# Three small rearrangements in a tuned linear-attention and feed-forward kernel: one state update earlier, one product and one mask moved to other engines

## The chip, the cores and the metric

The kernel runs on one core of a Trainium2 chip. The metric is the device time of one execution in microseconds (us). The profiler's span is some 1.7 to 1.9 us shorter than that time; spans are compared with spans and times with times. All executions here are of the state called fast (in the record their mean granted clock lies between 0.991 and 1.000). The engines are named as the profile names them: PE (TensorE matmuls), PEld (its weight loads), DVE (VectorE), ACT (ScalarE), POOL (GpSimd), and SP, whose queue (SPq) issues the DMA transfers.

## The reference, cut to what matters

```python
# batch 4, 8 heads, 768 positions, head_dim 64; causal linear attention with a decay per head
for b in range(nb):
    intra = einsum('bhic,bhjc->bhij', qb, kb) * Dmask          # scores inside the block, masked
    intra = einsum('bhij,bhjd->bhid', intra, vb)
    inter = einsum('bhid,bhde->bhie', qb * lam_pow, kv_state)  # earlier blocks, through the state
    out[:, :, sl] = intra + inter
    kv_state = lam_block * kv_state + einsum('bhsd,bhse->bhde', kb * rev_pow, vb)
# then a bilinear feed-forward on x = out, 3072 tokens of 512: (x @ w_a * (x @ w_b)) @ w_out, d_ff = 1536
```

## The kernel before

The 3072 tokens are cut into 24 units of 128 (6 per batch entry). For each unit the kernel multiplies q and k by decay factors (into a tile `qk`), transposes them (`qkT`; on PE up to unit 10, by a DMA transpose from unit 11), takes scores `kq`, masks them (`m`), adds intra and inter parts in PSUM (`o_ps`) and evacuates the sum as `xT`, the input of the feed-forward. The feed-forward runs over groups of 4, 1, 2, 4, 4, 4, 4 and 1 units, numbered from 0; while PE works on a group, a plan drops pieces of later units' attention into numbered slots between its matmuls. The order on every engine is fixed by the program.

```python
GROUPS = (4, 1, 2, 4, 4, 4, 4, 1)
PLAN = { ...
    2: [(0, "V", 6), (1, "T", 7), (1, "P", 8), (4, "T", 8), (5, "P", 9), (6, "S", 7),
        (6, "S", 8), (7, "V", 7), (8, "P", 10), (10, "T", 9), (11, "T", 10),
        (12, "Q", (7, 8, 9, 10)), (12, "P", 11), (13, "V", 9), (14, "P", 12),
        (14, "O2", (9, 10))],
    3: [(3, "S", 11), (3, "S", 12)], ... }
# groups 3, 4, 5 (u = 11, 15, 19): (1,"P",u+2) (3,"P",u+3) (4,"V",u) (7,"Q",(u,..,u+3)) (10,"P",u+4) ...
# P prepares a unit, T transposes on PE, S scores and masks, V updates the state,
# O2/Q finish two units (Q also takes the scores of two more)

def prep_k(u):
    early = u < n0 + 3                              # n0 = 4
    make_ks(u, "dve" if early else "pool")          # k times decay
    make_qs(u, "pool")                              # q times decay
    used["u"] = u + 1                               # lets pump() issue loads up to three units ahead
    if u >= DMA_T_FROM:                             # 11
        qkT = qkT_pool.tile(...)
        nc.sync.dma_start_transpose(out=qkT..., in_=U[u]["qk"]...)   # in the SP queue, in program order

def pieces_O(us, nxt=()):                           # O2 and Q
    ...inter(u) for us; scores(u) for nxt; intra(u) and evac_o(u) for us...
    if len(us) == 2 and us[0] >= n0 + 3:
        kv_beside(us[1])                            # eight half-width matmuls into the one state bank
    for u, kq in zip(nxt, kqs):
        masks(u, kq)                                # DVE, four masks
    if len(us) == 2 and us[0] >= n0 + 3 and us[1] % NB < NB - 1:
        kv_copy(us[1], kv["ps"])                    # DVE, behind the masks
```

## Time and profile before

| | before |
|---|---|
| median of the 3 runs given with it | 236.69 us (236.5 to 237.27) |
| median of 6 runs, with the 3 measured beside the changed kernel | 236.56 us (236.32 to 237.27) |
| span of the profiled execution | 234.5 us |
| PE, DVE, ACT, POOL busy | 96%, 49%, 40%, 21% |
| PE waits on lines that the change touches | 0.9 us (state copy), 0.3 us (ab product) |

The table is read with one question in mind: an engine other than PE matters only where PE waits for it. The columns are start, busy time, engine, line, operation, output from inputs, tile and shape, and the number of instructions; an idle time ahead of a row would follow in brackets.

```profile
99.75 1.03 PE L428 MATMUL b_ps<-xT,wb_sb 128*128 128x512 bf16 x4
100.62 0.39 PE L336 MATMUL o_ps<-qkT,st 128*128 128x128 bf16 x4
100.94 0.62 PE L309 MATMUL kq<-qkT 64*128 64x128 bf16 x16
101.49 0.64 PE L346 MATMUL o_ps<-m,vb 128*64 128x128 bf16 x16
```

The sixteen scores at 100.94 belong to units 13 and 14 and read what two DMA transposes wrote. No idle time is noted, so both had landed. By how much is not in this view: a list of waits shows only the transfers that came too late, never those that were just in time. The margin can be asked for. Unit 14's transpose was issued here:

```profile
94.87 2.20 SPq L281 DMA_TRANSPOSE qkT<-qk  x1
```

The view of the tile qkT for the stretch from 94.5 to 96 us gives 6.2 us from issue to landing, so it landed near 101.1. PE came to unit 14's scores, the second eight of the sixteen, at 101.17: the margin was below 0.1 us.

### The profile page before, as it was taken

What the parts mean: (1) busy time and instruction counts of PE and PEld (TensorE: products, weight loads), DVE (VectorE), ACT (ScalarE), POOL (GpSimd) and SP (SyncE); (2) the same over time, 40 slices, a digit from 0 to 9 for tenths busy, and PEclk for the clock granted to TensorE, in tenths of its full rate; (3) what the DMA queues carried; (4) which work ended last, traced back from release to release, by engine and by line L of the source; (5) the groups of instructions that cost most, each with busy time, mean ns of one, the idle gap of its engine ahead of it and who ended that gap; (6) DMA issues with size and microseconds to landing.
All of it is one profiled execution on the core that took longest, in us unless ns stands there. A gap on an engine that the chain in (4) does not pass through costs nothing.

```text
span 234.5 us, 4593 instructions
## 1 busy us (share of the span) xinstructions
PE 226.2 (96%) x1798; PEld 125.8 (54%) x1798; DVE 115.6 (49%) x205; ACT 92.9 (40%) x174; POOL 48.6 (21%) x63
## 2 busy tenths in 40 slices
PE   7699999999999899999999999999999999999994
PEld 2474444459688554454544454544454544444493
DVE  0896557637459644874144574135574224332050
ACT  3576753066463532242143242242341233431161
POOL 6041000254345453130333330030300000000000
PEclk9999999999999999999999999999999999999999
DMA  4999999999999999999819959515040220000311
GB/s 155 300 285 348 347 366 289 295 213 272 230 244 187 224 198 250 210 161 240 177 48 219 184 73 238 143 64 115 0 48 0 89 87 7 0 3 3 131 48 45
DMA packets 94278, 38.31 MB, mean 163 GB/s; under 512 B 81201, under 2 KB 89777, under 8 KB 94257
## 3 DMA queue, kind: packets, MB, share of 16 engines
q1 hardware_dynamic: 94112, 38.02, 72.1%
q8 instruction: 14, 0.23, 0.4%
q14 instruction: 8, 0.06, 0.1%
q10 hardware_dynamic: 144, 0.00, 0.0%
HBM read 28.32 MB, written 6.29 MB: 148 GB/s over the span
## 4 chain that ended last, share of the span: by engine, by line
PE 90%; DMA 3%; ACT 3%; DVE 2%; issue 1%; SPq 1%; DVEq 0%; ACTq 0%
PE a_ps L428 27%; PE b_ps L428 26%; PE op L449 26%; DMA k<-in_k_dram 3%; PE kq L309 2%; PE o_ps L346 2%; PE o_ps L336 2%; PE kvd L360 1%; PE tps L295 1%; ACT xT L353 1%; ACT o_sb L444 1%; DVE m L321 1%; SPq L207 1%; ACT st L390 1%; PE kq L561 1%
## 5 line engine op out<-in xcount | busy, mean ns | idle before, releaser
L440 DVE TENSOR_TENSOR ab<-a_sb,b_ps 128x512 bf16<-128x512 bf16 (+2 forms) x96 | 52.6, 553 | 80.6 <-PE b_ps L428 58.6
L428 PE MATMUL a_ps<-xT,wa_sb 128*128 128x512 bf16 (+2 forms) x384 | 77.1, 326 | 0.9 <-ACT xT L353 0.6
L428 PE MATMUL b_ps<-xT,wb_sb 128*128 128x512 bf16 (+2 forms) x384 | 77.2, 326 | 0.0
L435 ACT CAST a_sb<-a_ps 128x512 bf16<-128x512 f32 (+2 forms) x96 | 45.6, 481 | 63.5 <-PE a_ps L428 62.0
L449 PE MATMUL op<-wo_sb,ab 128*128 128x512 bf16 (+2 forms) x312 | 65.6, 363 | 0.0
L428 PEld LDWEIGHTS <-wb_sb 128*128 128x128 bf16 x384 | 34.5, 98 | 28.7
L428 PEld LDWEIGHTS <-wa_sb 128*128 128x128 bf16 x384 | 33.8, 98 | 29.4 <-issue 0.9
L449 PEld LDWEIGHTS <-ab 128*128 128x128 bf16 x312 | 28.7, 98 | 29.8
L321 DVE TENSOR_TENSOR m<-kq,lotri 128x512 bf16<-128x512 f32 x48 | 29.9, 683 | 19.3 <-PE kq L309 18.8
L257 POOL TENSOR_TENSOR qk<-kf,lp_k 128x512 bf16<-128x512 f32 x17 | 18.0, 1061 | 77.5 <-issue 31.6
L444 ACT COPY o_sb<-op 128x512 f32<-128x512 f32 (+2 forms) x26 | 14.2, 554 | 37.9 <-PE op L449 37.9
L262 POOL TENSOR_TENSOR qk<-qf,lp_q 128x512 bf16<-128x512 f32 x20 | 21.7, 1083 | 23.0 <-DMA qf<-in_q_dram 23.0
L353 ACT CAST xT<-o_ps 128x512 bf16<-128x512 f32 x23 | 12.5, 590 | 17.5 <-PE o_ps L346 17.4
L392 DVE TENSOR_TENSOR st<-kvd,bdiag 128x512 bf16<-128x512 f32 x18 | 12.3, 684 | 4.9 <-PE kvd L360 3.8
L297 ACT COPY qkT<-tps 128x1024 bf16<-128x1024 bf16 x7 | 7.1, 1012 | 10.4 <-PE tps L295 10.4
L195 PE MATMUL idle<-idle_sb 128*128 128x128 bf16 (+1 forms) x34 | 7.2, 348 | 1.3 <-DVE idle_sb L190 1.3
L271 DVE CAST vb<-vf 128x512 bf16<-128x512 f32 x17 | 8.3, 490 | 0.0
L271 POOL CAST vb<-vf 128x512 bf16<-128x512 f32 x7 | 4.8, 681 | 16.0 <-DMA vf<-in_v_dram 16.0
L346 PE MATMUL o_ps<-m,vb 128*64 128x128 bf16 x192 | 7.9, 222 | 0.0
L336 PEld LDWEIGHTS <-st 128*128 128x128 bf16 x80 | 5.4, 98 | 2.8
L309 PE MATMUL kq<-qkT 64*128 64x128 bf16 x160 | 6.6, 218 | 0.0
L346 PEld LDWEIGHTS <-vb 128*64 128x64 bf16 x192 | 5.8, 109 | 1.4
(54 smaller groups left out, 84.0 us busy)
## 6 DMA issues: line engine op xcount, KB each, us to landing
vf<-in_v_dram SPq DMA_DIRECT2D x24, 256.0 KB, 5.0
out_dram<-o_sb SPq DMA_DIRECT2D x23, 256.0 KB, 2.2
qf<-in_q_dram SPq DMA_DIRECT2D x20, 256.0 KB, 4.7
kf<-in_k_dram SPq DMA_DIRECT2D x20, 256.0 KB, 5.1
wst<-in_moe_w_a_dram SPq DMA_DIRECT2D x6, 512.0 KB, 8.7
wst<-in_moe_w_b_dram SPq DMA_DIRECT2D x6, 512.0 KB, 8.8
wst<-in_moe_w_out_dram SPq DMA_DIRECT2D x6, 512.0 KB, 8.5
q<-in_q_dram SPq DMA_DIRECT2D x2, 512.0 KB, 5.5
```

The source lines that it names most:

```text
L257: eng_of(eng).tensor_mul(qk[:, 1], raw.pop((u, "k")), lp_k[:, u % NB].to_broadcast([128, H, D]))
L262: eng_of(eng).tensor_mul(U[u]["qk"][:, 0], raw.pop((u, "q")), lp_q[:, u % NB].to_broadcast([128, H, D]))
L271: eng_of(eng).tensor_copy(vb, vf)
L321: nc.vector.tensor_mul(m, kq[i], lotri_bc)
L346: nc.tensor.matmul(d["o"][p, hp, :], lhsT=d["vb"][:, 2 * hp + i, :], rhs=d["m"](i, hp), start=(first and hp == 0), stop=True, skip_group_c ...
L353: nc.scalar.copy(xT[:, :, col:col + BLK], o_ps)
L392: nc.vector.tensor_mul(st[:].rearrange("p hp i d -> p hp (i d)"), ps[:].rearrange("p hp i d -> p hp (i d)"), bdiag_bc)
L428: nc.tensor.matmul(ps[:, :gt], lhsT=w_sb[:, s, f * 128:(f + 1) * 128], rhs=xT[:, s, :gt], start=(s == 0), stop=(s == KS - 1))
L435: nc.scalar.copy(a_sb[:, :gt], ps[:, :gt])
L440: nc.vector.tensor_mul(ab[:, f, :gt], a_sb[:, :gt], ps[:, :gt])
L444: nc.scalar.copy(o_sb[:, lo:hi], op[:, lo:hi])
L449: nc.tensor.matmul(op[:, lo:hi], lhsT=ab[:, f, t * 128:(t + 1) * 128], rhs=wo_sb[:, f, lo:hi], start=(f == 0), stop=(f == FC - 1))
```

## The change

The intent: PE waits in group 2 because unit 8's state copy stands behind four masks on DVE, so unit 8 gets its update alone, two slots earlier; in group 1 unit 6's k product leaves DVE; and in the opening one of eight masks is spread over ACT and POOL, unit 1's result is evacuated by DVE instead of ACT, and three idle-filling matmuls go.

```diff
--- before.py
+++ after.py
@@ -44,7 +44,7 @@
     1: [(0, "V", 4), (2, "T", 5), (3, "PK", 6), (6, "PV", 6), (6, "S", 5), (7, "T", 6),
         (10, "S", 6), (12, "O2", (5, 6)), (13, "P", 7)],
     2: [(0, "V", 6), (1, "T", 7), (1, "P", 8), (4, "T", 8), (5, "P", 9), (6, "S", 7),
-        (6, "S", 8), (7, "V", 7), (8, "P", 10), (10, "T", 9), (11, "T", 10),
+        (6, "S", 8), (7, "V", 7), (8, "P", 10), (10, "T", 9), (10, "V", 8), (11, "T", 10),
         (12, "Q", (7, 8, 9, 10)), (12, "P", 11), (13, "V", 9), (14, "P", 12),
         (14, "O2", (9, 10))],
     3: [(3, "S", 11), (3, "S", 12)],
@@ -272,8 +272,7 @@
         U[u]["vb"] = vb
 
     def prep_k(u):
-        early = u < n0 + 3
-        make_ks(u, "dve" if early else "pool")
+        make_ks(u, "dve" if u < n0 + 2 else "pool")
         make_qs(u, "pool")
         used["u"] = u + 1
         if u >= DMA_T_FROM:
@@ -314,11 +313,16 @@
         ms = mask(kq)
         U[u]["m"] = lambda i, hp: ms[i][:, hp, :]
 
-    def mask(kq):
+    def mask(kq, split=False):
         ms = []
         for i in range(2):
             m = msk_pool.tile([128, HP, 128], BF16, name=f"m{i}", tag=f"m{i}")
-            nc.vector.tensor_mul(m, kq[i], lotri_bc)
+            if split and i == 1:
+                raw_kq = scr[0][:, 8:9, :].rearrange("p s (h j) -> p (s h) j", h=HP)
+                nc.scalar.copy(raw_kq, kq[i])
+                nc.gpsimd.tensor_mul(m, raw_kq, lotri_bc)
+            else:
+                nc.vector.tensor_mul(m, kq[i], lotri_bc)
             ms.append(m)
         return ms
 
@@ -412,11 +416,11 @@
             intra(u)
             xT, col = xTs[u]
             evac_o(u, xT, col)
-        if len(us) == 2 and us[0] >= n0 + 3:
+        if len(us) == 2 and us[0] >= n0 + 5:
             kv_beside(us[1])
         for u, kq in zip(nxt, kqs):
             masks(u, kq)
-        if len(us) == 2 and us[0] >= n0 + 3 and us[1] % NB < NB - 1:
+        if len(us) == 2 and us[0] >= n0 + 5 and us[1] % NB < NB - 1:
             kv_copy(us[1], kv["ps"])
 
 
@@ -564,7 +568,7 @@
                                          start=True, stop=True, skip_group_check=True)
             kqs.append(kq)
         for up, kq in zip(ups, kqs):
-            ms4[i, up] = mask(kq)
+            ms4[i, up] = mask(kq, split=(i == 1 and up == 1))
 
     for u in range(n0):
         U[u] = dict(kn=kn4[:, u], qT=xT4["q"][:, :, u * BLK:(u + 1) * BLK],
@@ -579,7 +583,8 @@
     for at, i, j in ((2, 0, 0), (3, 0, 1), (4, 1, 0)):
         scale4("k", i, j)
         part_k(i, j, at)
-        warm(3)
+        if i == 0:
+            warm(3)
     scale4("k", 1, 1)
     for u in range(n0):
         make_vb(u, "pool")
@@ -608,7 +613,7 @@
     evac_o(0, *xTs[0])
     intra(1, True)
     inter(1)
-    evac_o(1, *xTs[1])
+    evac_o(1, *xTs[1], eng="dve")
     intra(2, True)
     intra(3, True)
     inter(2)
```

## The prediction

> **What bounds the kernel now.** I read the page first, then the waits of the tensor engine, then busy time by stage, then the timeline around each wait. The page puts PE far ahead of the rest, and the chain that ended last is almost all PE:
>
> ```profile
> PE 226.2 (96%) x1798; PEld 125.8 (54%) x1798; DVE 115.6 (49%) x205; ACT 92.9 (40%) x174; POOL 48.6 (21%) x63
> ...
> PE 90%; DMA 3%; ACT 3%; DVE 2%; issue 1%; SPq 1%; DVEq 0%; ACTq 0%
> ```
>
> So work taken from DVE, ACT or POOL is worth nothing by itself. Only three things shorten the run: PE work removed, a PE wait removed, or an earlier start of the steady part. The table by stage (stretch and its length, then busy us and instruction count of PE, PEld, DVE, ACT and POOL) says where waits are left:
>
> ```profile
> 0.00:18.73 18.73, 15.06 (x183) 9.56 (x184) 11.94 (x21) 10.77 (x20) 7.32 (x23) 1.00 0.95 253
> ...
> 51.92:62.90 10.98, 10.71 (x164) 8.82 (x164) 6.67 (x19) 6.13 (x17) 3.54 (x4) 1.00 1.02 254
> 62.90:86.15 23.25, 22.39 (x263) 17.29 (x262) 15.54 (x30) 11.45 (x22) 12.14 (x12) 1.00 1.15 208
> 86.15:212.80 126.65, 126.65 (x838) 62.26 (x837) 57.87 (x94) 42.78 (x74) 20.52 (x20) 1.00 0.59 113
> ```
>
> From 86 to 213 us PE has no gap at all, so a microsecond won before 86 should arrive at the end untouched. Before that the waits of PE are few, and two of them sit on lines that the change touches (columns: total us, times, longest):
>
> ```profile
> PE kvd L360 <- DVE st L392: 0.9, 1, 0.9
> ...
> PE a_ps L428 <- ACT xT L353: 0.6, 2, 0.5
> ...
> PE a_ps L428 <- DVE ab L440: 0.3, 1, 0.3
> ```
>
> The chain in order of time (start, length, what) shows each. In the opening, three idle-filling matmuls stand directly ahead of the scores; later four state copies and three xT casts on ACT stand ahead of the first feed-forward matmul:
>
> ```profile
> 11.47 0.17 PE idle L195 x3
> 11.64 0.55 PE kq L561 x16
> ...
> 17.08 1.60 ACT xT L353 x3
> 18.68 0.04 issue
> 18.73 1.89 PE a_ps L428 x8
> ...
> 55.54 0.40 DVE qk L257
> ...
> 56.14 0.29 DVE ab L440
> ...
> 80.16 1.28 DVE m L321 x2
> 81.44 0.61 DVE st L392
> 82.05 0.04 issue
> 82.09 0.38 PE kvd L360 x4
> ```
>
> At 55.5 us unit 6's k on DVE stands between two ab products, and PE waits for the second. At 82.1 us unit 9's state update waits until DVE has done four masks (units 9 and 10) and only then unit 8's state copy, which holds the one state bank.
>
> [...] POOL's k products have a mean of 1061 ns and its q products 1083. [...] the vb cast on DVE takes 421 ns at the median and 822 at most, and the timeline shows the 0.8 us ones beside a POOL product. [...] The trace shows only 112 ns against 98 per load in the half-width update, and eight of those cost PE about what four full-width ones cost (both 0.22 us, below).
>
> **The change, part by part.**
>
> Opening. The three idle matmuls go: 0.17 us from the chain. The DMA that landed k at 10.30 and the DVE scaling behind it do not move, so everything from the scores on moves by 0.17. DVE then does seven masks in place of eight. They follow each other every 0.61 us (eight take 4.88 from 12.07), so the seventh starts near 15.5 and ends near 16.2, and unit 2's state copy runs from about 16.15 to 16.8 instead of 16.87 to 17.55. The eighth mask goes ACT then POOL: the ACT copy (0.59 for this shape) fits in ACT's 0.99 us idle time before the first state copy, near 14.4 to 15.0; POOL is free at 15.66 after the fourth vb cast, whose DMA does not move, and multiplies until about 16.7. PE reaches the first matmul that reads this mask near 16.8, so it is just in time. ACT then has two xT casts instead of three; the last, unit 3's, now waits for PE's own inter matmuls (end 18.05 before, 17.88 here) and ends near 18.5 instead of 18.68. The first weights are cast by POOL until 17.76 + 0.62 = 18.38, held by a DMA, so no more than 0.3 can be won here. Gain: **0.2 us**.
>
> Unit 6's k to POOL. It takes 0.69 us from DVE and adds 1.05 to POOL, which is idle for 2.06 us from 51.8 and 1.37 from 54.5. POOL would do k and q of unit 6 by about 54.5, and PE's transposes want them at 56.9. The ab product moves from 56.14 to about 55.6. PE's scores before it start at 55.81 and take 0.33 in the chain, so the next matmul could start at 56.14 instead of 56.48. Gain: **0.34 us** (0.27 of it shown as idle, the rest is the refill of the pipeline, where the chain has 0.38 for the first four matmuls against 0.22 for later ones).
>
> Unit 8's update alone at slot 10. Added there: four full-width matmuls; for unit 7 the chain shows these as 0.22 us. Removed at slot 12: eight half-width ones, between 79.55 and the next matmul at 79.77, so 0.22. The PE work cancels. The state copy (0.68 us on DVE) moves from behind the masks to near 76.6, where DVE has caught up with PE and waits 0.24 us for the next product. Unit 9's update can then start when PE has issued its six matmuls from 79.77: 6 x 0.216 = 1.30, so at 81.07 instead of 82.09. Gain: **1.0 us at most**. What may be given back: after the masks DVE has unit 11's vb cast and then unit 9's copy, which the next inter needs near 82.8; if POOL starts unit 13's k, released by the same unit-9 update, just ahead of that cast, [...]. By the two gains upstream DVE comes 0.5 us earlier while unit 13's data land when they did, so I think DVE wins; I take off 0.15.
>
> Sum: 0.2 + 0.34 + 0.85 = 1.4 us. 236.69 - 1.4 = 235.3.
>
> **Rivals.** (a) The new wait: POOL's mask comes late and holds units 2 and 3, as it has a margin of only 0.1 us. For it: three engines in a row. Against: each had idle time there. It would cancel the 0.2 and at worst add 0.2: 235.6. (b) PE waits for unit 9's copy instead of unit 8's[...]: 0.85 falls to 0.4 or so: 235.8. (c) DMA bounds stretches 1 and 2 (its share is 1.02 and 1.15 there) so that an earlier PE only waits for data. Against: no wait of PE on DMA is in the list. If true, 0.5 us of the gain goes: 236.0. [...]
>
> **Range and chances.** The three gains are independent and their sum lies between 0.6 (b with half of a) and 1.6. Three runs of before spread over 0.8 us, so the median can move by 0.2. I predict 235.3, range 234.7 to 236.2. Faster by over 2% would need 4.7 us, more than PE waits for in all after the opening; slower by over 2% needs a clock loss or a long stall that no view suggests: 0.01 each, 0.98 within 2%.
>
> **What would show it right or wrong.** First feed-forward matmul at 18.5, not 18.73 (opening); no PE wait on ab near 56 and POOL's extra k before 54 (unit 6); no PE wait of 0.9 us on the state copy, and unit 9's update following the output matmuls without a gap, with all later times earlier by 1.4 (unit 8). A PE wait on the POOL mask, on unit 9's copy beside a 0.8 us vb cast, or on a qkT of unit 6 would be the rival that I undervalued.

What the trace shows: three of the 17 casts of values on DVE (at 70.45, 75.18 and 83.12 us) started while a POOL product ran, and took 0.81 to 0.82 us in place of 0.42, so 0.40 more. The 0.15, and in rival (b) the 0.4, are estimates. What the prediction calls the refill of the pipeline is a measured difference: four matmuls behind a wait show as 0.38 us in the chain (at 51.92, 56.48 and 82.09), the next four at 52.30 and 56.86 as 0.22. The granted clock of the opening is 1.00 in the traces of both kernels.

## The result, and the profile after

The changed kernel takes 235.64 us (median of 6 runs, 235.39 to 236.08) against 236.56 us for the kernel before. The ratio is 0.996, with a 95% interval of 0.9944 to 0.9976. Ratios here are the mean time of one kernel's fast runs over that of the other's of the same rounds, so not quite the ratio of the medians. The gain of the medians is 0.92 us where 1.4 were predicted.

First the page and PE's waits of the changed kernel (for the waits: total us, times, longest):

```profile
PE 226.4 (97%) x1791; PEld 125.6 (54%) x1791; DVE 114.5 (49%) x204; ACT 93.0 (40%) x174; POOL 49.6 (21%) x65
...
PE 88%; DMA 6%; ACT 2%; DVE 1%; SPq 1%; issue 1%; DVEq 0%
```

```profile
PE kq L308 <- DMA qkT<-qk: 1.3, 1, 1.3
```

Both waits that the change aimed at are gone, and a new one of 1.3 us has come, for a DMA. The share of DMA in the chain has doubled from 3% to 6%. The stages, cut at the same times as before, show where (the columns are those of the table in the prediction):

```profile
62.90:86.15 23.25, 23.25 (x263) 17.77 (x262) 14.24 (x30) 12.50 (x24) 12.31 (x12) 1.00 1.05 206
86.15:212.80 126.65, 125.33 (x832) 61.49 (x830) 58.44 (x95) 41.61 (x73) 20.52 (x20) 1.00 0.59 113
```

PE is now busy through the stretch up to 86 us and has a gap of 1.32 us in the long stretch that had none. The chain in order of time (start, length, what) tells the rest:

```profile
18.56 1.89 PE a_ps L432 x8
...
55.71 0.33 PE kq L308 x8
56.04 0.33 PE a_ps L432 x4
...
79.21 1.40 PE op L453 x6
80.61 0.22 PE kvd L364 x4
80.83 1.29 PE op L453 x6
...
84.67 0.86 PE a_ps L432 x4
...
94.77 0.25 SPq L126
95.14 5.84 DMA qkT<-qk
101.02 0.40 PE kq L308 x8
...
102.31 0.86 PE a_ps L432 x4
```

The same places in the chain of the kernel before:

```profile
63.27 0.44 PE a_ps L428 x4
...
86.31 0.86 PE a_ps L428 x4
...
102.46 0.86 PE a_ps L428 x4
```

Read the one against the other. The first feed-forward matmul starts at 18.56 instead of 18.73. At 56.04 PE goes straight from scores to the next a_ps. At 80.61 unit 9's update follows the output matmuls without a gap. Group 3 starts at 84.67 instead of 86.31: PE leads by 1.64 us. Then unit 14's DMA transpose, issued at 95.14, lands 5.84 us later and holds the second eight of the scores until 101.02. The next a_ps starts at 102.31 in the chain, against 102.46 before. In this execution 0.15 us of the lead is left. It was the slowest of its six (236.08 us), and the traced execution of the kernel before was the fastest of its six (236.32), which is why the spans, 234.4 and 234.5, hardly differ.

The lead by group, from the starts of the first a_ps of a group in the chains (opening; group 1 from 51.92 to 63.27 before and 51.76 to 62.75 after; group 2 from there to 86.31 and 84.67): 0.17, 0.36 and 1.12 us. Two of these belong in part to the single execution. Six traces with the changed opening have their first feed-forward matmul at 18.54 to 18.68, and four with the old one (the kernel before, experiments 4, 6 and 10) at 18.68 to 18.78, so 0.17 is near the scatter. And group 2 took 23.04 us in the trace of the kernel before, where DVE's cast of unit 9's values took 0.82 us in place of 0.42; in four later traces with the same group 2 (experiments 4, 5, 6 and the detour alone) it took 22.83 to 22.84. Against these the changed kernel's group is 0.91 us shorter, not 1.12.

### The profile page after: what moved, and what is told of

Read it like the earlier page. It is cut to its first block, busy times and chain, and to the rows that moved or that the text cites. A ratio compares the mean times of both kernels' runs of the same rounds, so it can differ in the third digit from the quotient of the medians.

```text
span 234.4 us, 4575 instructions
## 1 busy us (share of the span) xinstructions
PE 226.4 (97%) x1791; PEld 125.6 (54%) x1791; DVE 114.5 (49%) x204; ACT 93.0 (40%) x174; POOL 49.6 (21%) x65
## 4 chain that ended last, share of the span: by engine, by line
PE 88%; DMA 6%; ACT 2%; DVE 1%; SPq 1%; issue 1%; DVEq 0%
PE op L453 26%; PE a_ps L432 26%; PE b_ps L432 25%; DMA k<-in_k_dram 3%; PE o_ps L350 3%; DMA qkT<-qk 2%; PE kq L308 2%; PE o_ps L340 2%; PE kvd L364 2%; PE tps L294 1%; DVE m L325 1%; ACT o_sb L448 1%; SPq L207 1%; PE kq L565 1%; ACT xT L357 0%
## 5 line engine op out<-in xcount | busy, mean ns | idle before, releaser
L325 DVE TENSOR_TENSOR m<-kq,lotri 128x512 bf16<-128x512 f32 x47 | 29.4, 682 | 19.0 <-PE kq L308 18.7
L257 POOL TENSOR_TENSOR qk<-kf,lp_k 128x512 bf16<-128x512 f32 x18 | 18.9, 1051 | 79.3 <-PE kvd L364 30.9
L262 POOL TENSOR_TENSOR qk<-qf,lp_q 128x512 bf16<-128x512 f32 x20 | 21.0, 1051 | 23.0 <-DMA qf<-in_q_dram 23.0
L357 ACT CAST xT<-o_ps 128x512 bf16<-128x512 f32 x22 | 12.0, 590 | 18.4 <-PE o_ps L350 17.9
L271 DVE CAST vb<-vf 128x512 bf16<-128x512 f32 x17 | 7.5, 441 | 0.0
```

Source lines behind the costliest of these rows:

```text
L257: eng_of(eng).tensor_mul(qk[:, 1], raw.pop((u, "k")), lp_k[:, u % NB].to_broadcast([128, H, D]))
L262: eng_of(eng).tensor_mul(U[u]["qk"][:, 0], raw.pop((u, "q")), lp_q[:, u % NB].to_broadcast([128, H, D]))
L271: eng_of(eng).tensor_copy(vb, vf)
L325: nc.vector.tensor_mul(m, kq[i], lotri_bc)
L357: nc.scalar.copy(xT[:, :, col:col + BLK], o_ps)
```

## The experiments

**Theory A:** on PE the change is worth what was predicted, and most of the missing part is given back to one transfer, unit 14's transpose. **Rival B:** transfers as a whole bound this stretch, so that with this wait gone the next transfer would stop PE. **Rival C:** the transpose is late because of what makes its data, not because of what stands ahead of it. Later, **theory D:** of the opening, only the idle matmuls count. (The expectations count loosely: their "third group" is group 3 of this text, their "second group" is group 1.)

**1. The wait taken away, every transfer left.** The scores of unit 14 read unit 13's tile. Its output is wrong, which doesn't matter for the time.

```diff
 def scores(u, kq=None):
-    d = U[u]
+    d = U[13 if u == 14 else u]
```

> The changed kernel, but the scores of unit 14 read unit 13's transposed q and k (wrong results on purpose). Every transfer stays as it is; only the wait for unit 14's DMA transpose at its first use is gone. Theory A (the change wins 1.6 us by the start of the third group, and this one wait gives 1.3 of it back in the trace): no PE wait on qkT near 100 us, every later time earlier by 1.0 to 1.5 us than in the changed kernel's trace, 234.7 to 235.1 us, so 1.5 to 1.8 under the kernel before. Rival B (the loads as a whole bound this stretch, and the next transfer would stop PE as well): another PE wait on a DMA after 101 us, and a time within 0.2 of the changed kernel, 0.8 to 1.0 under the kernel before.

Measured: 234.69 us (234.58 to 234.73, 5 runs), ratio 0.9919 (0.9907 to 0.9932), beside 236.65 for the kernel before in these rounds. No wait of PE on a DMA is left in the trace. Rival B falls: behind this transfer there is room. The spread of 0.15 us is far below the 0.69 of the changed kernel.

**2. The transpose moved up in the queue.** This is the order of issues in the changed kernel (start, time that the issue took, line, kind, what), then with unit 16's three loads put behind unit 14's transpose. There the x2 is unit 13's and unit 14's transposes together; unit 14's own issue starts at 92.07:

```profile
90.83 1.67 SPq L280 DMA_TRANSPOSE qkT<-qk  x1
92.55 0.60 SPq L126 DMA_DIRECT2D qf<-in_q_dram  x1
93.20 0.70 SPq L126 DMA_DIRECT2D kf<-in_k_dram  x1
94.01 1.02 SPq L126 DMA_DIRECT2D vf<-in_v_dram  x1
95.14 2.32 SPq L280 DMA_TRANSPOSE qkT<-qk  x1
```

```profile
90.58 3.04 SPq L281 DMA_TRANSPOSE qkT<-qk  x2
93.67 0.57 SPq L126 DMA_DIRECT2D qf<-in_q_dram  x1
```

```diff
 def prep_k(u): ...
-    used["u"] = u + 1
+    if u != 13:
+        used["u"] = u + 1       # unit 16's loads are let go by unit 14, after its transpose
```

> The changed kernel with the three loads of unit 16 put behind unit 14's DMA transpose in the SP queue instead of ahead of it; right results. Theory A with the queue's order as the cause: the transpose is issued near 92.5 us instead of 95.1, lands near 98, PE does not wait, and the time is that of the run that does not read it, 234.7 to 235.1 us. Rival C (the transpose is held by POOL's products of unit 14 or is slow in itself, not by what stands ahead of it): it still lands near 101 and the time stays at 0.8 to 1.0 under the kernel before.

Measured: 234.69 us (234.53 to 234.73, 5 runs), results right, ratio 0.9919 (0.9905 to 0.9932). The transpose landed near 96.1, 4.0 us after its issue, in place of 101.0. Rival C falls as well. The data of the transpose had been ready long before: in the changed kernel POOL's q product for unit 14 starts at 88.28 and takes 1.04 us, so from 89.32 on the transpose waited only for its turn. In the queue there stood ahead of it unit 13's transpose, whose issue took 1.67 us, and the three loads with 0.60, 0.70 and 1.02. PE with the transpose ahead:

```profile
98.98 0.39 PE L341 MATMUL o_ps<-qkT,st 128*128 128x128 bf16 x4
99.30 0.62 PE L309 MATMUL kq<-qkT 64*128 64x128 bf16 x16
99.85 0.64 PE L351 MATMUL o_ps<-m,vb 128*64 128x128 bf16 x16
```

These are the rows shown of the kernel before at 100.62 to 101.49, now 1.64 us earlier, and again without a bracket.

**3. PE comes later instead.** The whole piece moves one slot on, in group 3 only.

```diff
-         (7, "Q", (_u, _u + 1, _u + 2, _u + 3)), ...
+         (8 if _g == 3 else 7, "Q", (_u, _u + 1, _u + 2, _u + 3)), ...
```

> The changed kernel with the attention piece of units 11 to 14 one slot later in the third group (slot 8 instead of 7, 1.73 us of PE work later); right results. Theory A: unit 14's transpose lands before PE comes to it, no wait, 234.7 to 235.1 us. Rival B: PE waits elsewhere and the time stays at 0.8 to 1.0 under the kernel before. A miss for both would be a new wait because the units' state copies and casts come later.

Measured: 234.64 us (234.56 to 234.69, 4 runs), results right, ratio 0.9917 (0.9904 to 0.9931). Three different ways of taking away one wait end within 0.05 us of each other.

Two readings over the traces of the two kernels and of all experiments, here and below (without two that fell on outliers, twelve traces), close the argument. In the six with the queue as it was, PE started group 3 anywhere from 84.65 to 86.31, yet the transpose was issued between 94.53 and 95.25 and landed between 100.4 and 101.3: its time does not follow PE's. And in all but experiment 3, where the piece was moved, the execution ended 135.04 to 135.16 us after PE started unit 14's scores, whether PE had waited for them or not. So behind this point nothing over 0.12 us is won or lost.

**4. Control: the same queue move on the kernel before.**

> Control: the kernel before with the same move of unit 16's loads behind unit 14's transpose. In its trace PE did not wait for that transpose, so theory A expects no change, within 0.2 us of the kernel before. If it is faster by 0.5 us or more, the move has a worth of its own and the run with the change and the move can't be read as the change's.

Measured: 236.07 us (236.03 to 236.24, 5 runs) against 236.65, ratio 0.9979 (0.9967 to 0.9992). This is a miss: it was to change nothing, as the trace of before shows no wait there. By its own expectation the move has a worth of its own, so a run with the change and the move can be compared with the control only, not with the kernel before. The kernel before runs from 236.08 to 236.76 in these rounds, and its fastest run is where the control always is. It fits that in most executions the kernel before is held by the same transfer for about half a microsecond: in the one that was traced the margin was below 0.1 us. A rival fits as well: a long cast at unit 9, as in that trace (0.82 us, with group 2 longer by 0.21) and again in experiment 10. The move comes after group 2 in program order, so why the control should be free of it is not shown. No trace of a slower execution of the kernel before was taken, so the two are not separated. What follows for the reckoning does not depend on it: without this transfer in the way, the change is worth 236.07 - 234.69 = 1.38 us.

**5 to 7. Each part alone on that control.** Their medians stand against its 236.07 us from the rounds above, as these rounds' runs of the kernel before scatter from 236.16 to 237.85. The record gives these rounds another chip number (2, against 10), and no control was run there; the medians of the kernel before agree (236.66 and 236.65), but there is no interval for these differences.

> One part alone, on the kernel before with unit 16's loads behind unit 14's transpose (236.07 us, tight, as that transpose no longer stops PE). This part: the opening (three idle matmuls gone, one mask over ACT and GpSimd, unit 1 evacuated by VectorE). The prediction gave it 0.2; the changed kernel's trace has the first feed-forward matmul 0.17 earlier. Expected 235.85 to 235.95 us.

> One part alone on the same base: unit 6's k on GpSimd. The prediction gave it 0.34; the changed kernel's trace has the second group (from its first feed-forward matmul to that of the next group) shorter by 0.36. Expected 235.65 to 235.8 us and no PE wait for the ab product. Rival: the wait of PE moves to another VectorE product in the same group and the time stays at 236.0 or more.

> One part alone on the same base: unit 8's update alone at slot 10. The prediction gave it at most 1.0 and put 0.85 into the sum; the changed kernel's trace has the group shorter by 1.12. Theory: 235.0 to 235.2 us, and no PE wait of 0.9 us for the state copy. Rival (VectorE's cast of unit 11's values meets GpSimd's product for unit 13 and delays unit 9's copy, as this kernel has no 0.5 us of lead from the other parts): a PE wait on the copy before unit 10's inter matmuls and 235.4 to 235.6 us.

The rival named in the last rests on the casts of 0.82 us in place of 0.42 beside a POOL product in the trace of the kernel before.

| part alone | edit | median us | against 236.07 | predicted |
|---|---|---|---|---|
| opening | all its lines of the diff | 235.87 (235.83 to 237.35) | 0.20 | 0.2 |
| unit 6's k on POOL | the `prep_k` lines | 235.66 (235.61 to 235.78) | 0.41 | 0.34 |
| unit 8 alone at slot 10 | the `PLAN` and `n0 + 5` lines | 235.21 (235.06 to 238.32) | 0.86 | 0.85 |

The sum is 1.47, near the 1.38 of all three together. The ratios to the kernel before are 0.9966, 0.9947 and 0.9948; the first and the last are pulled up by an outlier each. The profile of unit 8's part fell on its outlier (span 236.5), where PE waited 2.3 us for q in the opening, so no start time is taken from it.

**8 and 9. Is the detour of the mask worth anything?** The same result was built without it (all masks on DVE, unit 1 evacuated by ACT; the idle matmuls out, unit 6, unit 8 and the transpose as in experiment 2), and the detour was tried alone on the control.

> The changed kernel with unit 14's transpose ahead (234.69 us) but with all masks of the first units on VectorE and unit 1 evacuated by ACT as before; the idle matmuls stay out. Theory D (the idle matmuls are all that the opening won; in the changed kernel's trace the last xT cast waits for PE's own chain, 0.17 earlier): same time within 0.1 us, 234.6 to 234.8. Rival (the detour over ACT and GpSimd is needed, as VectorE would hold units 2 and 3): the first feed-forward matmul comes back to 18.7 us and the time to 234.85 to 234.9.

Measured: 234.71 us, but 234.55 to 237.05, with the profile on the slowest run, where PE waited 3.6 us for q's scaling. It was repeated:

> The changed kernel with unit 14's transpose ahead, without the detour of the mask and of unit 1's evacuation, once more, because its profiled execution had q land late. Theory D: first feed-forward matmul at 18.5 to 18.6 us when q lands near 5.9, and 234.6 to 234.8 us; the rival 18.65 to 18.75 and 234.85 to 234.9.

Measured: 234.66 us (234.56 to 234.72, 6 runs), right results, first feed-forward matmul at 18.62. The detour alone:

> On the kernel before with unit 14's transpose ahead (236.07 us): only one mask over ACT and GpSimd and unit 1 evacuated by VectorE, the idle matmuls kept. Theory D (the detour wins nothing, the idle matmuls are all): first feed-forward matmul at 18.65 to 18.73 us and 236.0 to 236.1. Rival (the detour has a worth of its own): first matmul at 18.5 and 235.85 to 235.9.

Measured: 236.05 us (235.99 to 236.23), first feed-forward matmul at 18.70. Theory D holds to within 0.1 us: the detour wins nothing that these runs can see, and the three idle matmuls are the opening's gain. This rests on the times; the starts scatter too much to tell. Lines from the timelines of ACT and POOL in the changed kernel say why:

```profile
17.93 0.59 ACT L357 CAST xT<-o_ps 128x512 bf16<-128x512 f32 x1 [0.41 <-PE o_ps L340]
```

```profile
15.63 1.16 POOL L323 TENSOR_TENSOR m<-scratch,lotri 128x512 bf16<-128x512 bf16 x1
```

The mask came in time, at 16.79, and ACT had one cast less; but the time it gained it spends waiting 0.41 us for PE, whose own matmuls feed the last cast. With three casts on ACT, as in the repeat of run 8, they end near 18.58, where with two the last ends at 18.52.

**10. Unit 8's part alone, with the transpose where it was.**

> Unit 8's update alone at slot 10, the only change to the kernel before, with unit 14's transpose where it was. On the base with the transpose ahead this part is worth 0.86 us (235.21). Theory A: here PE reaches unit 14 about 1 us earlier than the transpose and waits, so most of it is given back: 235.5 to 236.1 us and a PE wait on qkT of 0.5 to 1.2. Rival (the transpose is in time unless all parts are in): 235.1 to 235.3 and no wait.

Measured: 236.5 us (235.75 to 236.9), against 236.59 for the kernel before; ratio 0.9978 (0.9936 to 1.0019), so no gain is shown. A part worth 0.86 us on the control shows almost nothing here. The trace has the wait, 0.49 us on qkT, at the low end of what was expected of it; the median time lies above what was expected, a miss. The rest was lost earlier, in group 2. These are DVE, then POOL, in that trace:

```profile
70.47 1.24 DVE L271 CAST vb<-vf 128x512 bf16<-128x512 f32 x1
71.63 0.41 DVE L440 TENSOR_TENSOR ab<-a_sb,b_ps 128x256 bf16<-128x256 bf16 x1
71.96 2.47 DVE L321 TENSOR_TENSOR m<-kq,lotri 128x512 bf16<-128x512 f32 x4
```

```profile
70.38 1.04 POOL L257 TENSOR_TENSOR qk<-kf,lp_k 128x512 bf16<-128x512 f32 x1 [2.35 <-DMA kf<-in_k_dram]
```

The cast of unit 9's values, 0.42 us by itself, took 1.24, as POOL's product for unit 10 had started 0.09 us ahead of it. The four masks behind it came late, and PE fell behind by about 0.6 us: the group took 63.29 to 85.83, or 22.54 us, against 21.92 in the first trace of the changed kernel. PE's list of waits does not show this loss: in the chain four groups of four matmuls behind 72.72 take 0.57 to 0.60 us each in place of 0.44. In the first trace of the changed kernel the same product started at 70.59, after the cast at 69.93, which took 0.42. This is the long cast that the prediction's rival (b) feared, met at another unit and larger than the 0.40 us that the trace of the kernel before shows (1.24 - 0.42 = 0.82). In these two traces the one that started first kept its time: here the product took its 1.04, and in the first trace of the changed kernel a cast that started at 81.79, 0.22 us ahead of a product, took 0.42 and the product 1.09. By its bracket above POOL had waited 2.35 us for unit 10's k, so here it hung on when that landed.

**11. The changed kernel once more, in the same rounds.**

> The changed kernel once more, in the same rounds. Theory A: 235.4 to 235.9 us with a PE wait on unit 14's qkT between 0.3 and 1.3, differing from run to run as the transpose lands earlier or later, so a wider spread than the 0.2 us of the kernels in which PE does not wait for it.

Measured: 235.92 us (235.51 to 236.22, 6 runs) against 236.59, ratio 0.9958 (0.9921 to 0.9994). Its trace has both effects: a cast of 1.28 us at 70.05, so PE leads less, and then a wait of only 0.54 us, up to the same 101.02 us as in the first trace:

```profile
101.02 0.40 PE L308 MATMUL kq<-qkT 64*128 64x128 bf16 x8 [0.54 <-DMA qkT<-qk]
```

Both traces end after 234.4 us, although PE arrived 0.78 us later in the second (the first eight scores start at 99.30 and at 100.08). The landing of the transpose set the end, not what PE had won or lost before it.

**The better version.** Experiments 2, 3 and 8 give right results and beat both kernels: 234.64 to 234.69 us, about 1.9 us below the kernel before and 1.0 to 1.3 below the changed one. The repeat of 8 is the simplest of them.

## Why the prediction was right or wrong

The time was within the range, 0.34 us above the point. That is partly luck: the range was made for rivals (a) and (b), while the missing time went to a transfer. (Its low end, a sum of 0.6, does not follow from its own figures either: (b) leaves 0.94, and half of (a) takes 0.1 to 0.2 from that.) By the steps of the prediction:

- **Opening, 0.2: right in size (0.20 alone; the trace's 0.17 is near the scatter), partly wrong in its cause.** The idle matmuls gave all that was measured. The prediction gave the shorter queue on ACT a small share; PE's chain took its place.
- **Unit 6, 0.34: right.** 0.36 in the trace, 0.41 alone, and the wait on ab is gone. POOL did unit 6's k at 52.41 and q from 53.42, and was done at 54.46, as named (54.5).
- **Unit 8, 0.85: right.** 0.86 alone, and 0.91 by the traces, with the long cast of the kernel before left out. The PE work cancels as said: the four full-width matmuls take 0.22 us in the chain; the eight half-width ones of unit 10's update show as 0.12, with the output matmuls behind them longer by 0.11 (1.40 against 1.29), so 0.23 together. DVE won the race for unit 11's cast (0.42 us, at 80.85). A cast was long beside a POOL product in some executions all the same, at unit 9 (1.24 us in experiment 10, 1.28 in 11).
- **The sum of 1.4: right for PE** (1.38 with the transfer out of the way).
- **"From 86 to 213 us PE has no gap at all, so a microsecond won before 86 should arrive at the end untouched": this step failed.** No gap was taken to mean room. Unit 14's transpose was just in time, and for a PE that came 1.64 us earlier it was 1.3 us late. The changed kernel (235.64 us in the first rounds) stands 0.95 us above what it has without that wait (234.69 in the second), and the kernel before 236.65 - 236.07 = 0.58 us above the control, so the change nets 0.4 to 0.5 us less than it wins. The second half of the step held: from unit 14's scores on, a gain arrived at the end untouched.
- **Rival (c), DMA, was named but weighed wrongly.** It was looked for in stretches 1 and 2 and dismissed because "no wait of PE on DMA is in the list". Its estimate, 236.0 us, is close to what the slower runs show.

What stays open: what sets the issue and the landing of the transpose (issue to landing 3.1 to 5.8 us over the 13 transposes in the changed kernel), and whether the kernel before is mostly held by it or by the long cast.

## What to carry to other kernels

A stage without gaps says that its inputs are on time, not that they would be on time for a faster start. Before adding up a gain that moves a whole stage earlier, find the transfers whose issue does not move with the engine, such as those in a queue of issues in program order (here unit 14's transpose, issued at 94.53 to 95.25 us whether PE started group 3 at 84.65 or at 86.31), and compare the landing with the new time of use. If a wait must be taken out, the cheap remedies are to put the urgent transfer ahead of loads that nobody needs yet, or to let the consumer come one slot later.
